# A two-layer FNet/H3 kernel: the work list of the 128-point stage is reordered, its short convolution is spread in even shares, and its constants are loaded one item ahead

## The chip, the cores and the metric

The kernel runs on one core of one Trainium2 chip. The metric is the time of the whole program on the device, in microseconds (us), lower is better. It is given as the median of several runs. One further execution was taken by the profiler, and all durations in this text come from it. The trace names the engines PE (matrix products), PEld (the weight loads beside them), DVE (element-wise work, two inputs), ACT (element-wise work, one input, and copies out of PSUM), POOL (a few very small operations and some DMAs) and SP (most DMAs).

## What is computed

```python
x = A_x                                        # 2048 x 576, f32
x = x + A_ref(layernorm(x), ...)               # y = Re(DFT_seq(DFT_hidden(x)))
x = x + B_ref(layernorm(x), B_k, B_v, ...)     # below
x = x + A_ref(layernorm(x), ...)
x = x + B_ref(layernorm(x), B_k, B_v, ...)

def B_ref(q, k, v, shift_k, ssm_k, ssm_D):
    k_shift = short causal convolution of k over 4 positions, per channel
    kv = k_shift * v
    y = long causal convolution of kv with ssm_k (FFT of 4096 points, per channel)
    return q * (y + kv * ssm_D)
```

The B branch but for its gate `q` doesn't depend on x: `kv` and its long convolution are computed once and used by both layers.

## The kernel before

The program is one unrolled list of instructions per engine. The author writes them in one order; the framework's scheduler may move an instruction within its engine's list, puts in all waits, and after that each engine runs its list strictly in order. An instruction that waits holds everything behind it on that engine; a DMA that waits on SP's list holds the DMAs behind it.

All products are f32 products in three terms: each operand is split into a rounded high part (written by ACT, line 92) and the remainder (a subtraction on DVE, line 93), called hi and lo below.

**Layer 1, A branch** (`layer`, line 296): for each of 4 column blocks and for the cosine and the sine matrix there are 16 steps. A step loads one 128x512 piece of the DFT matrix (`load_c`, line 213), splits it (hi on ACT and lo on DVE, into tiles called `mats`), and issues 14 products of 128x512 into four PSUM banks `s` and one bank `rm`. During the first 16 steps it also needs row block j of the normalised x. Blocks 8 to 15 go through a chain (`sums`, line 612, and `normed_x`, line 638): ACT sums (L615), DVE scales (L616), ACT squares (L617), DVE scales (L618), POOL raises to a power (L619), DVE multiplies (L641), ACT scales (L642), ACT rounds (L195), DVE forms the remainder (L197, L198). After 16 steps the four banks are copied out and split again (tiles `u`).

**The 128-point stage** of the long convolution (`branch`, line 343) is interleaved with these steps by hand: lines 736 to 744 take pieces of it, about two half items per step, until step 42. It works off a list `todo` (lines 394 and 395) of 32 items, (j, 1) for row block j of the kernel `ssm_k` and (j, 0) for row block j of the signal `kv`. For an item

- `f1_loads` (line 398) issues its input from SP (`land`, three tiles) and, if j is new, the constants of j (`fc`, five tiles, 256 KB) from POOL (line 170); it runs two items ahead (line 448);
- `f1_split` (line 415): a signal is first multiplied by v (DVE, line 419); then hi on ACT and lo on DVE (tile `f1r`);
- `f1_products` (line 427): 12 products of 128x288, copied out by ACT (line 436) and stored to DRAM from ACT's list (line 437). From item 8 on the products lag two items behind the split.

The order before is: items (1,1), (0,1), (2,1), (3,1), then signals 0 to 3, then (j,0), (j,1) in turn for j from 4 on.

The signals need the short convolution (`convolve`, line 377), made in pairs of row blocks: a pair is 7 DVE operations on 128x1152 (four products, L386, three additions, L391; a product is cut in two of 128x576 where its rows wrap around). Lines 449 to 456 decide how many of them go out in each half item: what is still owed for the next signal that lacks rows, divided by the halves until then, rounded up.

PSUM has three banks for these products (`bk`). The stage after it (tiles `mid`, from step 45 on) reads back what this stage stored.

Of the kernel before, what the change touches and what calls it, by code (L numbers as in the profile page):

```python
# [12 lines left out]
AF = mybir.ActivationFunctionType  # L13
OP = mybir.AluOpType

P = 128
S = 2048
D = 576
J = S // P
# [8 lines left out]
EARLY = 6  # L28
ROWS = (0, 1, 2, 3, 4, 5, 6, 7, 8, 9)
K_FIRST = 4  # L30
F1_16 = 5
F1_LAG = 8
F1_END = 42
# [32 lines left out]
def fnet_h3_kernel(ctx: ExitStack, tc: tile.TileContext, x, c_mat, w_re, w_im, k_pad, v, shift_k,  # L66
# [101 lines left out]
    def load_fr(dst, src):  # L168
        with tc.issue_after(pows[-1]):
            nc.gpsimd.dma_start(dst, src)  # L170
# [169 lines left out]
    def quads(v):  # L340
        return v.rearrange("p (a q) -> p a q", a=4)

    def branch():
# [33 lines left out]
        def convolve():  # L377
            for i in range(J // 2):
                if not wt:
                    load_w4()  # L380
                load_k(i + KR - 1)
                rp = rows[i] = two(ring["rp"]())
                for t in range(4):
                    out_t = two(tmp) if t else rp
                    for n, k in k_rows(2 * i + t):
                        nc.vector.tensor_tensor(out_t[:, n], k, wt[3 - t][:, n], OP.mult)  # L386
                    yield
                    if t == 1:
                        load_k(i + KR)
                    if t:  # L390
                        nc.vector.tensor_tensor(rp, rp, out_t, OP.add)  # L391
                        yield

        todo = [(1, 1), (0, 1)] + [(j, 1) for j in range(2, K_FIRST)] + [(j, 0) for j in range(K_FIRST)]
        todo += [(j, src) for j in range(K_FIRST, J) for src in range(2)]
        loads = [0]

        def f1_loads(upto):
            while loads[0] < min(upto, len(todo)):
                j, src = todo[loads[0]]  # L400
                loads[0] += 1
                if j not in fcs:
                    fcs[j] = quads(ring["fc"]())
                    if pows:
                        load_fr(fcs[j], f1c[j])
                    else:
                        raw = quads(tmp[:, :4 * P])
                        nc.sync.dma_start(raw, f1c[j])
                        nc.scalar.activation(fcs[j], raw, AF.Copy)
# [27 lines left out]
                nc.scalar.dma_start(t_d[hf][:, j, :, src, :], so)  # L437
                yield

        conv, made_ops, split_up = convolve(), 0, []  # L440
        for n, (j, src) in enumerate(todo):
            f1_loads(n + 1)
            if n < 2:
                yield
            split_up.append((j, src, f1_split(j, src), fcs[j]))
            products = f1_products(*split_up.pop(0)) if len(split_up) > (1 if n < F1_LAG else 2) else iter(())
            if n:
                f1_loads(n + 3)
            later = [m for m in range(n + 1, len(todo)) if todo[m][1] == 0 and 7 * (todo[m][0] // 2 + 1) > made_ops]
            for half in range(2):  # L450
                next(products, 0)
                if later and n > 1:
                    left = 7 * (todo[later[0]][0] // 2 + 1) - made_ops
                    for _ in range(-(-left // (2 * (later[0] - n) - half)) if left > 0 else 0):
                        next(conv)
                        made_ops += 1
                yield
        next(conv, 0)
        for left_over in split_up:
# [646 lines left out]
```

## Time and profile before

| | us |
|---|---|
| runs before: median of 3 (lowest, highest) | 1201.36 (1199.54, 1201.96) |
| the profiled execution, its own time | 1199.98 |
| its span, from first to last instruction | 1198.1 |
| busy PE, DVE, ACT, POOL | 1177.1, 838.9, 633.9, 75.1 |
| the clock that PE was granted | 0.999 |

The profiled execution is 1.4 us faster than the median and inside the range of the runs; 1.9 us of its time lies outside the span. A row of the timeline gives start, duration, engine, line, operation, tiles and the count that was merged, and in brackets the idle time before it and who ended it. PE's products are pipelined, so a row's duration ends after the next one has begun; losses are best read from one start to the next.

### The profile page before, as it was taken

What the parts mean: (1) busy time and instruction counts of PE and PEld (TensorE: products, weight loads), DVE (VectorE), ACT (ScalarE), POOL (GpSimd) and SP (SyncE); (2) the same over time, 40 slices, a digit from 0 to 9 for tenths busy, and PEclk for the clock granted to TensorE, in tenths of its full rate; (3) what the DMA queues carried; (4) which work ended last, traced back from release to release, by engine and by line L of the source; (5) the groups of instructions that cost most, each with busy time, mean ns of one, the idle gap of its engine ahead of it and who ended that gap; (6) DMA issues with size and microseconds to landing.
All of it is one profiled execution on the core that took longest, in us unless ns stands there. A gap on an engine that the chain in (4) does not pass through costs nothing.

```text
span 1198.1 us, 18264 instructions
## 1 busy us (share of the span) xinstructions
PE 1177.1 (98%) x6320; PEld 1026.9 (86%) x6320; DVE 838.9 (70%) x1495; ACT 633.9 (53%) x1266; POOL 75.1 (6%) x116
## 2 busy tenths in 40 slices
PE   7999999999999999999999999999999999999997
PEld 6888888988888888889988898888888888889997
DVE  7889983679877677775447766875676777764764
ACT  7965665467766667665435666544444435440200
POOL 2210000000000000001101121000000000001111
PEclk9999999999999999999999999999999999999999
DMA  9879998546766657658967686872772677794621
GB/s 345 285 241 309 287 288 271 169 128 199 207 191 191 215 164 215 205 141 242 314 203 236 221 258 213 273 259 71 216 272 83 206 277 273 227 353 145 222 88 41
DMA packets 146111, 261.96 MB, mean 219 GB/s; under 512 B 15841, under 2 KB 44769, under 8 KB 146018
## 3 DMA queue, kind: packets, MB, share of 16 engines
q1 hardware_dynamic: 102674, 205.58, 53.9%
q10 hardware_dynamic: 36432, 42.63, 10.2%
q0 software_dynamic: 6912, 12.59, 4.0%
q8 instruction: 50, 0.82, 0.3%
q14 instruction: 43, 0.35, 0.1%
HBM read 194.09 MB, written 66.65 MB: 218 GB/s over the span
## 4 chain that ended last, share of the span: by engine, by line
PE 71%; ACT 3%; DVE 3%; DMA 2%; issue 1%; ACTq 0%; POOLq 0%; DVEq 0%
PE s L75 39%; PE bk L75 28%; PE rm L75 4%; ACT flts L490 2%; ACT mid L490 1%; DMA flts<-in_c_mat 1%; DVE mid L496 1%; DMA flts<-t 1%; DMA flts<-vd 1%; DVE u L93 1%; DMA ph<-in_c_mat 0%; DVE mats L93 0%; ACT mats L92 0%; DVE flts L510 0%; DVE flts L269 0%
## 5 line engine op out<-in xcount | busy, mean ns | idle before, releaser
L75 PE MATMUL s<-mats 128*128 128x512 f32 x2088 | 528.7, 392 | 0.8 <-DVE u L93 0.5
L75 PEld LDWEIGHTS s<-mats 128*128 128x128 f32 x2088 | 380.9, 188 | 70.5 <-DVE u L93 1.3
L92 ACT ACTIVATE mats<-flts 128x512 fp32r<-128x512 f32 x206 | 128.4, 626 | 96.1 <-PE bk L75 32.5
L93 DVE TENSOR_TENSOR mats<-flts,mats 128x512 fp32r<-128x512 f32 x206 | 141.1, 688 | 53.4 <-ACT mats L92 50.8
L490 ACT ACTIVATE flts<-bk 64x288 f32<-64x288 f32 (+1 forms) x288 | 115.9, 406 | 103.1 <-PE bk L75 85.0
L496 DVE TENSOR_TENSOR mid<-flts,mid 128x576 fp32r<-128x576 f32 (+1 forms) x160 | 102.0, 638 | 47.9 <-ACT mid L490 44.0
L75 PE MATMUL bk<-mid 128*128 128x288 f32 x768 | 128.5, 298 | 3.3 <-ACT flts L490 2.2
L75 PEld LDWEIGHTS bk<-mid 128*128 128x128 f32 x768 | 114.8, 188 | 19.6 <-ACT flts L490 8.1
L75 PE MATMUL bk<-w,u 128*128 128x288 f32 x864 | 120.2, 295 | 0.8 <-DVE flts L283 0.7
L75 PEld LDWEIGHTS bk<-w,u 128*128 128x128 f32 x864 | 117.4, 188 | 3.9 <-DVE flts L283 1.5
L490 ACT ACTIVATE mid<-flts 128x576 fp32r<-128x576 f32 (+1 forms) x159 | 87.1, 581 | 14.9 <-DMA flts<-vd 9.6
L75 PE MATMUL rm<-mats 128*128 128x512 f32 x304 | 94.7, 390 | 0.0
L436 ACT ACTIVATE flts<-bk 128x288 f32<-128x288 f32 x128 | 49.0, 410 | 46.5 <-PE bk L75 39.2
L75 PEld LDWEIGHTS bk<-f1r 128*128 128x128 f32 x384 | 59.5, 192 | 14.8 <-ACT f1r L92 6.9
L75 PE MATMUL bk<-f1r 128*128 128x288 f32 x384 | 65.0, 301 | 7.3 <-ACT f1r L92 6.4
L75 PE MATMUL bk<-mats 128*128 128x288 f32 (+1 forms) x376 | 67.8, 317 | 0.0
L75 PEld LDWEIGHTS rm<-mats 128*128 128x128 f32 x304 | 56.9, 188 | 11.8
L283 DVE TENSOR_TENSOR flts<-flts,bk 128x288 f32<-128x288 f32 x48 | 21.8, 453 | 63.8 <-PE bk L75 63.6
L75 PE MATMUL s<-t,mats 128*128 128x512 f32 x264 | 64.9, 389 | 0.0
L184 POOL TENSOR_TENSOR flts<-flts 128x1 f32<-128x1 f32 x35 | 29.6, 845 | 523.8 <-DVE flts L183 523.8
L75 PE MATMUL bk<-mats,t 128*128 128x288 f32 (+1 forms) x368 | 59.3, 303 | 0.0
L75 PEld LDWEIGHTS bk<-mats 128*128 128x128 f32 x376 | 55.6, 188 | 3.4
(148 smaller groups left out, 1429.7 us busy)
## 6 DMA issues: line engine op xcount, KB each, us to landing
flts<-in_c_mat SPq DMA_DIRECT2D x148, 256.0 KB, 3.6
ph<-in_c_mat SPq DMA_DIRECT2D x54, 512.0 KB, 4.2
t<-flts ACTq DMA_DIRECT2D x64, 288.0 KB, 4.4
flts<-t SPq DMA_DIRECT2D x64, 288.0 KB, 3.0
flts<-in_c_mat SPq DMA_DIRECT2D x30, 512.0 KB, 5.1
vd<-flts ACTq DMA_DIRECT2D x64, 144.0 KB, 2.8
flts<-vd SPq DMA_DIRECT2D x32, 288.0 KB, 4.8
mid<-in_i2c POOLq DMA_DIRECT2D x32, 256.0 KB, 4.9
```

What stands on the lines that cost most here:

```text
L75: nc.tensor.matmul(ps, lhsT, rhs, start=first, stop=last, skip_group_check=more)
L92: a = nc.scalar.activation(h, src, AF.Copy).ins
L93: return a, nc.vector.tensor_tensor(l, src, h.bitcast(F32), OP.subtract).ins
L184: pows.append(nc.gpsimd.tensor_tensor(rs, ve, mhalf, OP.pow).ins)
L283: added[:] = [nc.vector.tensor_tensor(r[:, cs], r[:, cs], ps[:, :HD], OP.add).ins]
L436: stored[:] = [nc.scalar.activation(so[:, c, :], ps[:, :HD], AF.Copy).ins]
L490: last_act.append(nc.scalar.activation(*args, **kw).ins)
L496: nc.vector.tensor_tensor(l, src, h.bitcast(F32), OP.subtract)
```

## The change

The list of items, what is loaded when, and the spreading of the convolution are changed. The order of items is now (1,1), (0,1), (2,1), (3,1), (0,0), (1,0), and then for j = 4, 5, ... 15 the kernel item (j,1) followed by the signal item (j-2,0), with signals 14 and 15 at the end. A signal j from 4 on so stands at place 2j+3 of the list, where it stood at 2j; a kernel item j at 2j-2, where it stood at 2j+1. From item 8 on, the constants of the item at hand and of the next one are requested behind the split, and no longer together with the input two items ahead. The convolution gets a running share: the largest debt per half over all coming signals is added at each half, and an operation goes out for each whole unit; a pair may not begin before the signal two pairs back has been used.

```diff
+K_AHEAD = 3
...
-        todo = [(1, 1), (0, 1)] + [(j, 1) for j in range(2, K_FIRST)] + [(j, 0) for j in range(K_FIRST)]
-        todo += [(j, src) for j in range(K_FIRST, J) for src in range(2)]
+        todo = [(1, 1), (0, 1)] + [(j, 1) for j in range(2, K_FIRST)] + [(0, 0), (1, 0)]
+        for j in range(K_FIRST, J):
+            todo += [(j, 1), (j - K_AHEAD + 1, 0)]
+        todo += [(j, 0) for j in range(J - K_AHEAD + 1, J)]
         loads = [0]
+
+        def f1_const(j):
+            if j not in fcs:
+                fcs[j] = quads(ring["fc"]())
+                if pows:
+                    load_fr(fcs[j], f1c[j])
+                else:
+                    raw = quads(tmp[:, :4 * P])
+                    nc.sync.dma_start(raw, f1c[j])
+                    nc.scalar.activation(fcs[j], raw, AF.Copy)
 
         def f1_loads(upto):
             while loads[0] < min(upto, len(todo)):
                 j, src = todo[loads[0]]
                 loads[0] += 1
-                if j not in fcs:
...
+                if j <= K_FIRST:
+                    f1_const(j)
                 landed[j, src] = ring["land"]()
...
-        conv, made_ops, split_up = convolve(), 0, []
+        conv, made_ops, split_up, share = convolve(), 0, [], 0.0
         for n, (j, src) in enumerate(todo):
             f1_loads(n + 1)
             if n < 2:
                 yield
-            split_up.append((j, src, f1_split(j, src), fcs[j]))
+            xf = f1_split(j, src)
+            if n > 7:
+                f1_const(j)
+                if n < len(todo) - 1:
+                    f1_const(todo[n + 1][0])
+            split_up.append((j, src, xf, fcs[j]))
...
                 if later and n > 1:
-                    left = 7 * (todo[later[0]][0] // 2 + 1) - made_ops
-                    for _ in range(-(-left // (2 * (later[0] - n) - half)) if left > 0 else 0):
+                    owed = [(7 * (todo[m][0] // 2 + 1) - made_ops, 2 * (m - n) - half) for m in later]
+                    share += max(left / halves for left, halves in owed)
+                    while share > 0.999 and made_ops < 7 * (J // 2):
+                        pair_at = made_ops // 7
+                        if pair_at > 1 and todo.index((2 * pair_at - 3, 0)) > n:
+                            break
                         next(conv)
                         made_ops += 1
+                        share -= 1
```

The number of instructions stays the same on every engine. What the scheduler makes of it differs from about 30 us of the span on, on PE between its products 112 and 766 of 6320 (up to 161 us); behind that PE's list is the same row by row. Three places follow, as the instructions stand in each engine's list; the new file's lines are one or more higher (L386 is now L387, L391 is L392, L419 is L426, L93 is L94).

First, DVE ahead of the `u` splits of block 0's first half, at 65 to 71 us of the trace. Before:

```order
L198 TENSOR_TENSOR mats<-early,mats 128x512
L93 TENSOR_TENSOR f1r<-f1f,f1r 128x576
L386 TENSOR_TENSOR f1f<-f1f 128x1152
L93 TENSOR_TENSOR mats<-flts,mats 128x512
L391 TENSOR_TENSOR f1f<-f1f 128x1152
L93 TENSOR_TENSOR mats<-flts,mats 128x512 x2
L93 TENSOR_TENSOR u<-s_66,u 128x512
```

and now:

```order
L199 TENSOR_TENSOR mats<-early,mats 128x512
L94 TENSOR_TENSOR f1r<-f1f,f1r 128x576
L94 TENSOR_TENSOR mats<-flts,mats 128x512
L392 TENSOR_TENSOR f1f<-f1f 128x1152
L94 TENSOR_TENSOR mats<-flts,mats 128x512 x2
L94 TENSOR_TENSOR u<-s_66,u 128x512
```

One operation of the convolution has gone from this stretch.

Second, DVE right behind the `u` splits, at 75 to 88 us of the trace. Before:

```order
L419 TENSOR_TENSOR f1f<-f1f,flts 128x576
L386 TENSOR_TENSOR f1f<-f1f 128x1152 x2
L93 TENSOR_TENSOR f1r<-f1f,f1r 128x576
L93 TENSOR_TENSOR mats<-flts,mats 128x512
L391 TENSOR_TENSOR f1f<-f1f 128x1152
L93 TENSOR_TENSOR mats<-flts,mats 128x512
L386 TENSOR_TENSOR f1f<-f1f 128x1152
L419 TENSOR_TENSOR f1f<-f1f,flts 128x576
L391 TENSOR_TENSOR f1f<-f1f 128x1152
L93 TENSOR_TENSOR mats<-flts,mats 128x512
L93 TENSOR_TENSOR f1r<-f1f,f1r 128x576
L386 TENSOR_TENSOR f1f<-f1f 128x576 x2
```

and now:

```order
L94 TENSOR_TENSOR f1r<-flts,f1r 128x576
L387 TENSOR_TENSOR f1f<-f1f 128x1152
L94 TENSOR_TENSOR mats<-flts,mats 128x512
L392 TENSOR_TENSOR f1f<-f1f 128x1152
L94 TENSOR_TENSOR mats<-flts,mats 128x512
L426 TENSOR_TENSOR f1f<-f1f,flts 128x576
L387 TENSOR_TENSOR f1f<-f1f 128x1152 x2
L94 TENSOR_TENSOR f1r<-f1f,f1r 128x576
L94 TENSOR_TENSOR mats<-flts,mats 128x512
L94 TENSOR_TENSOR f1r<-flts,f1r 128x576
L392 TENSOR_TENSOR f1f<-f1f 128x1152
L94 TENSOR_TENSOR mats<-flts,mats 128x512
```

Ahead of the third split of a matrix piece (`mats`) here stood five convolution operations and two products with v; now there are four and one.

Third, DVE in the chain of the normalised row blocks, at 33 to 39 us of the trace (128x1 rows are the chain's scalars, L641 now L658 is the one behind POOL's power). Before:

```order
L618 TENSOR_SCALAR flts<-flts 128x1
L616 TENSOR_SCALAR flts<-flts 128x1
L93 TENSOR_TENSOR f1r<-flts,f1r 128x576
L641 TENSOR_TENSOR flts<-flts 128x1
L391 TENSOR_TENSOR f1f<-f1f 128x1152
L93 TENSOR_TENSOR mats<-flts,mats 128x512
L618 TENSOR_SCALAR flts<-flts 128x1
L386 TENSOR_TENSOR f1f<-f1f 128x1152
L616 TENSOR_SCALAR flts<-flts 128x1
L197 TENSOR_TENSOR mats<-early,mats 128x64
L198 TENSOR_TENSOR mats<-early,mats 128x512
```

and now:

```order
L635 TENSOR_SCALAR flts<-flts 128x1
L392 TENSOR_TENSOR f1f<-f1f 128x1152
L635 TENSOR_SCALAR flts<-flts 128x1
L658 TENSOR_TENSOR flts<-flts 128x1
L633 TENSOR_SCALAR flts<-flts 128x1
L658 TENSOR_TENSOR flts<-flts 128x1
L94 TENSOR_TENSOR mats<-flts,mats 128x512
L635 TENSOR_SCALAR flts<-flts 128x1
L658 TENSOR_TENSOR flts<-flts 128x1
L198 TENSOR_TENSOR mats<-early,mats 128x64
L199 TENSOR_TENSOR mats<-early,mats 128x512
```

Three of the chain's L658 now stand ahead of the row block that these rows end with, where one L641 stood; each waits for POOL.

More of the change, by code (lines that the diff above doesn't have):

```diff
@@ L401, in f1_loads @@
                 loads[0] += 1
-                if j not in fcs:
[L403 to L409, printed above, removed]
+                if j <= K_FIRST:
+                    f1_const(j)
                 landed[j, src] = ring["land"]()
```

## Prediction

> **What bounds the kernel now.** I read the page first (busy time of each engine, then the cost of the products that the change moves), then the stretches by windows, then PE's list of waits, and last PE's timeline, to see what single waits the stage has.
>
> ```profile
> span 1198.1 us, 18264 instructions
> PE 1177.1 (98%) x6320; PEld 1026.9 (86%) x6320; DVE 838.9 (70%) x1495; ACT 633.9 (53%) x1266; POOL 75.1 (6%) x116
> L75 PE MATMUL bk<-f1r 128*128 128x288 f32 x384 | 65.0, 301 | 7.3 <-ACT f1r L92 6.4
> ```
>
> PE is busy for 1177.1 of 1198.1 us, so whatever another engine gains can show only where PE stands still; all its idle time together is 21.0 us. The products of the reordered stage (bk from f1r) have 7.3 us of idle time ahead of them.
>
> ```profile
> PE bk L75 <- ACT f1r L92: 6.4, 2, 5.9
> 32.60:66.20 33.60, 33.60 (x160) 28.24 (x159) 27.34 (x63) 30.34 (x65) 9.61 (x10) 1.00 0.79 254
> 66.20:96.20 30.00, 29.27 (x147) 24.20 (x146) 28.39 (x36) 14.58 (x33) 1.58 (x3) 1.00 0.81 262
> 96.20:126.20 30.00, 30.00 (x165) 26.29 (x164) 29.57 (x33) 18.18 (x42) 1.58 (x3) 1.00 1.01 328
> ```
>
> Of those 7.3 us the first row explains 6.4, and 5.9 of that is one wait: the program's start, before the point from which the lists differ. What is left for this change is small. The windows (their columns are the busy time of PE, PEld, DVE, ACT and POOL, the granted clock, the DMA share and GB/s) cover most of the stretch in which the lists differ: PE counts as idle for only 0.73 us, all of it between 66.2 and 96.2. DVE is what stands behind PE: 28.39 of 30.00 there and 29.57 in the next window. The granted clock is 1.00 throughout, so no term is needed for it.
>
> Idle time as the trace counts it misses what hides in the overlap of pipelined products. So I count from one start to the next.
>
> ```profile
> 67.69 1.22 PE L75 MATMUL bk<-f1r 128*128 128x288 f32 x8
> 68.75 2.00 PE L75 MATMUL s<-mats 128*128 128x512 f32 x8
> 70.59 0.39 PE L75 MATMUL rm<-mats 128*128 128x512 f32 x1
> 71.26 3.01 PE L75 MATMUL s<-mats 128*128 128x512 f32 x12 [0.28 <-DVE u L93]
> ...
> 79.46 1.59 PE L75 MATMUL bk<-f1r 128*128 128x288 f32 x9
> 80.89 2.00 PE L75 MATMUL s<-mats 128*128 128x512 f32 x8
> ...
> 83.18 2.43 PE L75 MATMUL s<-mats 128*128 128x512 f32 x10
> 86.05 0.53 PE L75 MATMUL bk<-f1r 128*128 128x288 f32 x2 [0.44 <-ACT f1r L92]
> 86.42 0.62 PE L75 MATMUL s<-mats 128*128 128x512 f32 x2
> ...
> 94.36 2.38 PE L75 MATMUL bk<-f1r 128*128 128x288 f32 x15
> 96.58 1.08 PE L75 MATMUL s<-mats 128*128 128x512 f32 x4
> ```
>
> The unit of a 128x512 product is (2.43 - 0.39) / 9 = 0.227 us (the row at 83.18: its length less one product's own, over the nine others), and of a 128x288 product (68.75 - 67.69) / 8 = 0.132 us. Against these units the stretch loses in six places that are worth counting: 70.59 to 71.26, 0.67 - 0.227 = **0.44**; inside the row at 71.26, 3.01 - 0.39 - 11 x 0.227 = **0.12**; 79.46 to 80.89, 1.43 - 9 x 0.132 = **0.24**; 83.18 to 86.05, 2.87 - 10 x 0.227 = **0.60**; 86.05 to 86.42, 0.37 - 0.26 = **0.11**; 94.36 to 96.58, 2.22 - 15 x 0.132 = **0.24**. Together **1.8 us**. That is what the change can win directly.
>
> **The change part by part.** No instruction is added or taken away, so the 1177 us of products stay; only places and requests move.
>
> ```profile
> L386 DVE TENSOR_TENSOR f1f<-f1f 128x1152 f32<-128x1152 f32 x5 | 6.7, 1345 | 0.0
> ```
>
> *Even shares of the convolution, and signals later.* This group is of DVE between 66.2 and 96.2 us: one convolution operation takes 1.35 us. Counted in the order of both kernels up to the split that stands at about 96 us in before, DVE has 12 operations' worth of convolution there now and 8 after: 4 x 1.35 = 5.4 us less, in a stretch where DVE's free time is 1.6 us. At the `u` copies (the first place in the section on the change) one operation fewer stands ahead, 1.35 us against a loss of 0.44 + 0.12: both go. What is late next there is ACT's copy of the four banks itself, which ends no later than before.
>
> ```profile
> 69.42 2.07 ACT L92 ACTIVATE u<-s 128x512 fp32r<-128x512 f32 x4 [2.40 <-DVE f1f L391]
> 84.80 0.63 ACT L92 ACTIVATE mats<-flts 128x512 fp32r<-128x512 f32 x1 [2.20 <-DMA flts<-in_c_mat]
> 78.20 0.33 SPq L365 DMA_DIRECT2D f1f<-in_k_pad  x1
> 79.51 2.16 SPq L166 DMA_DIRECT2D flts<-in_c_mat  x2
> ```
>
> The loss at 86.05 (0.60 + 0.11) comes through three queues. PE waits for ACT's f1r; right ahead of that, at 84.80, ACT has a matrix piece for which it stood 2.20 us, since its load hadn't landed; SP could issue that load only at 79.51, because the k_pad load in front of it (78.20) had to wait for a tile that DVE's convolution frees. With DVE 5.4 us lighter the tile is free earlier, and the k_pad load sits further back. I take 0.71 as gone. If that cover fails, it stays, and no more. The two losses on bk's own groups (0.24, 0.24) end on banks that ACT hasn't copied out; ACT is 14.58 of 30.00 busy there and waits for DVE and for loads, so I take them as gone too, though this is the weakest of the terms.
>
> *Order of the items.* A kernel item needs no convolution, so PE has 12 products at hand that depend on SP and ACT and one DVE split alone. Their number to 161 us is the same. Price nothing; hidden under it is the extra lag, which only makes the stored results of signals later by three places. The stage that reads them begins after all of them are issued in both kernels.
>
> *Constants one item ahead.*
>
> ```profile
> 89.40 0.53 POOL L170 DMA_DIRECT2D f1r<-in_f1c  x1 [7.53 <-PE bk L75]
> 99.44 0.53 POOL L170 DMA_DIRECT2D f1r<-in_f1c  x1 [9.51 <-PE bk L75]
> f1r<-in_f1c POOLq DMA_DIRECT2D x15, 256.0 KB, 5.4
> ```
>
> POOL issues a block's constants when PE frees a tile, here 10.0 us apart (89.40 to 99.44), thus 5.0 us per item; they land 5.4 us after the issue. Block j is now requested at item 2j - 3 and first read by the products of item 2j - 2, which lag two items: three items, 15 us, against 5.4. The tile (of five) was last read by signal j - 5, issued five items before that. Nothing waits, price 0. Without this cover one landing of 5.4 us would show at each block; it needs items of under 1.8 us. POOL's only other work in that stretch is the powers below, and the request that moved ahead of three of them costs its 0.53 us in POOL's list, under DVE's work.
>
> *What is put in front of something else.* The third place in the section on the change adds: two more of the chain's waits for POOL stand on DVE ahead of a normalised row block's remainder (L198), and behind it the splits of matrix pieces queue, for which PE waits.
>
> ```profile
> 54.48 0.16 DVE L641 TENSOR_TENSOR flts<-flts 128x1 f32<-128x1 f32 x1 [0.66 <-POOL flts L619]
> 54.69 0.69 DVE L198 TENSOR_TENSOR mats<-early,mats 128x512 fp32r<-128x512 f32 x1
> 56.10 2.45 PE L75 MATMUL s<-mats 128*128 128x512 f32 x10
> 62.23 0.68 DVE L198 TENSOR_TENSOR mats<-early,mats 128x512 fp32r<-128x512 f32 x1
> 64.36 1.75 PE L75 MATMUL s<-mats 128*128 128x512 f32 x7
> ```
>
> A wait for POOL costs DVE 0.66 where nothing stands between; two are 1.32. The block's remainder at 54.69 ends at 55.38 and its first reader is the second product of the row at 56.10, thus at 56.33: a slack of 0.95. At 62.23 it is 64.36 - 62.91 = 1.45. Pushed by 1.32 the first is 1.32 - 0.95 = 0.37 late, the second not. I take **0.4** as added. The ends: 0, since DVE has 33.60 - 27.34 = 6.3 us free in that window and the moved convolution operation (1.35) pays for the push; and 3 x 0.66 = 2.0, if three blocks lose a wait each. I stay near the lower end because its rows are nearest.
>
> **Sum**: -1.8 + 0.4 = -1.4 us. Against the profiled execution's own 1199.98 that is 1198.6. That execution is 1.4 below the median of 1201.36; the same step from the median gives **1199.9**, which I predict.
>
> **The rivals.**
>
> *F, faster.* Two waits behind the stage go as well.
>
> ```profile
> 217.72 0.64 PE L75 MATMUL s<-mats 128*128 128x512 f32 x2
> 218.76 0.92 PE L75 MATMUL bk<-w,u 128*128 128x288 f32 x5 [0.41 <-DVE flts L283]
> PE bk L75 <- DVE flts L283: 0.7, 2, 0.4
> ```
>
> The first, between the two rows, is 1.04 - 2 x 0.227 = 0.59 where the trace counts 0.41 idle; the list of waits has 0.7 for both, so the second (near 224 us) is by the same ratio 0.3 x 0.59 / 0.41 = 0.4, together 1.0. For it: SP's load of the matrix w now stands three places earlier. Against it: every list is the same from 161 us on, and these end on DVE work that follows PE's own pace. With no loss at the row blocks: -1.8 - 1.0 = -2.8, 1198.6.
>
> *N, the change doesn't do what it says.* PE's stalls only change place: the losses on bk's groups and at 86.05 end on loads (2.20 us for in_c_mat) and on banks, and with a DMA share of 1.01 between 96.2 and 126.2 us, the transfers and not DVE may set when those come. Then the 1.8 us appear again as waits for transfers, at 96 to 161 us: 1201.4. Against it: PE counts no idle time in that window.
>
> *S, slower.* The chain of the row blocks becomes what PE waits for, at 33 to 64 us: each of the eight blocks 8 to 15 shows a POOL wait of 0.66 to PE, 8 x 0.66 = 5.3, net -1.8 + 5.3 = +3.5, 1204.9. It decides from the point where the slack of each block is below 0.66. For it: ACT is 30.34 of 33.60 busy in that window, and powers take longer beside DVE:
>
> ```profile
> 36.86 1.59 POOL L619 TENSOR_TENSOR flts<-flts 128x1 f32<-128x1 f32 x1 [2.21 <-DVE flts L618]
> 53.89 0.55 POOL L619 TENSOR_TENSOR flts<-flts 128x1 f32<-128x1 f32 x1 [2.13 <-DVE flts L618]
> 36.70 1.35 DVE L386 TENSOR_TENSOR f1f<-f1f 128x1152 f32<-128x1152 f32 x1
> ```
>
> A power takes 0.55 beside an idle DVE and 1.59 beside a convolution operation. Against it: it then ends at 38.45, 0.40 behind DVE's operation (38.05), so DVE has worked meanwhile and its wait doesn't grow; and the two slacks above are 0.95 and 1.45.
>
> [...]
>
> **How the numbers follow.** Forecast 0.48 (its terms rest on rows of the stretch, but the step is small), F 0.22, N 0.14, S 0.16. About 0.2% of 1201.36, 2.4 us, is what a measurement of this kernel can tell from no change, so faster means below 1198.96 and slower above 1203.76. F lies below; of the forecast, whose runs scatter by half of 1201.96 - 1199.54 = 1.2 us, a quarter (0.12) does too: faster 0.34. S is slower: 0.16. The rest, 0.36 + 0.14, is the same: 0.50. The range takes in F less that scatter, 1198.6 - 1.2 = 1197.4, and, above, the upper end at the row blocks (-1.8 + 2.0, 1201.6) with the same scatter, 1202.8; N lies inside, S is left out with some 0.03 of tails.
>
> **What would show it.** After the change PE's timeline between 66 and 100 us should have no step over 0.1 us above the units; DVE between 75 and 96 us should show convolution operations apart, not two or three together; POOL's waits for PE ahead of its constants should be shorter, and no PE wait should name DMA f1r. The wait for DVE u at 71.26 should be gone. The forecast is wrong if PE shows waits for mats of L198 or L195 (S), if the waits at 218 and 224 us are gone (F), or if new ones stand between 96 and 161 us (N).

## The result and the profile after

| | us |
|---|---|
| before: median of 22 runs (lowest, highest) | 1200.1 (1196.94, 1203.59) |
| changed: median of 22 runs (lowest, highest) | 1196.92 (1194.13, 1201.16) |
| ratio, 95% interval | 0.9976 (0.9969 to 0.9983) |
| changed, the profiled execution: time, span | 1198.31, 1196.5 |

The change makes the kernel faster by 0.24%, 2.9 us (2.0 to 3.7). The prediction was 1.4 us less, 1199.9; the median is 1196.92. The direction was right and the size was not. What failed is the sum: it holds +0.4 at the row blocks that wasn't there, nothing for about 1.1 us outside the reordered stretch, and it starts from a median of three runs (1201.36) that 22 runs put at 1200.1.

The page of the changed kernel, beside that of before, shows the same work and a span that is 1.6 us shorter; the windows, of the same stretches as before, show where PE no longer stands still:

```profile
span 1196.5 us, 18260 instructions
PE 1176.5 (98%) x6320; PEld 1027.8 (86%) x6320; DVE 840.1 (70%) x1495; ACT 636.3 (53%) x1266; POOL 73.0 (6%) x116
```

```profile
32.60:66.20 33.60, 33.60 (x160) 28.25 (x159) 27.85 (x63) 31.34 (x68) 8.42 (x10) 1.00 0.81 260
66.20:96.20 30.00, 30.00 (x156) 25.91 (x155) 28.91 (x36) 17.37 (x38) 1.14 (x3) 1.00 0.92 289
96.20:126.20 30.00, 30.00 (x164) 26.25 (x163) 29.57 (x33) 16.81 (x37) 1.58 (x3) 1.00 0.98 310
```

In the second window PE is busy for all 30.00 us and starts 156 products instead of 147. DVE is as busy as before (28.91 against 28.39, and 29.57 in both kernels in the third). That is the first sign that the forecast's reason, a lighter DVE, is not the whole story.

PE's timeline of the changed kernel, at the places that answer to those shown of before:

```profile
70.16 0.61 PE L76 MATMUL rm<-mats 128*128 128x512 f32 x2
70.61 1.08 PE L76 MATMUL bk<-f1r 128*128 128x288 f32 x7
71.53 2.89 PE L76 MATMUL s<-mats 128*128 128x512 f32 x12
...
83.23 1.52 PE L76 MATMUL s<-mats 128*128 128x512 f32 x6
84.59 0.95 PE L76 MATMUL bk<-f1r 128*128 128x288 f32 x6
85.38 1.53 PE L76 MATMUL s<-mats 128*128 128x512 f32 x6
...
92.02 0.96 PE L76 MATMUL bk<-f1r 128*128 128x288 f32 x6
92.83 1.55 PE L76 MATMUL s<-mats 128*128 128x512 f32 x6
```

Six products of 128x512 in 84.59 - 83.23 = 1.36 are 0.227 each; six of 128x288 in 85.38 - 84.59 = 0.79 are 0.132 each: the units of before. The row at 71.53 follows the seven at 70.61 after 0.92 = 7 x 0.132: the wait for `u` is gone. And the products of this stage stand in groups of three, six and seven, where before had nine and fifteen in a row at these places.

For all kernels below I add up, in such stretches of PE's list, what each start comes later than the unit after the start in front of it ("loss"), by the numbers of the products. Products 111 to 250 run at about 33 to 63 us, 250 to 400 at 63 to 94, 400 to 520 at 94 to 116. Each kernel's own first profile is the first number:

| loss in us, products | 111-250 | 250-400 | 400-520 | 4500-5600 |
|---|---|---|---|---|
| before, four profiles | 0.10, 0.10, 0.63, 0.14 | 1.74, 2.25, 1.49, 0.99 | 0.50, 0.50, 0.50, 0.50 | 1.47, 0.96, 1.33, 1.71 |
| changed, four profiles | 0.07, 0.06, 0.06, 0.06 | 0.20, 0.20, 0.20, 0.21 | 0.31, 0.31, 0.32, 0.31 | 0.70, 0.31, 0.40, -0.11 |

Over products 111 to 520 that is 2.36 in the mean before and 0.58 now: **1.8 us** won where the change acts. Start and stages between scatter by more than that from one execution to the next: the first 111 products lose 3.0 to 5.5 us in these eight profiles, products 1000 to 1200 1.2 to 4.3. The mean span of the four profiles is 1198.0 before and 1195.9 now. A single pair of profiles can't carry a statement about one microsecond of the whole; the stretch can, since it repeats.

### The profile page after: what moved, and what is told of

Same layout as the page of the kernel before. It is cut to its first block, busy times and chain, and to the rows that moved or that the text cites. A ratio compares the mean times of both kernels' runs of the same rounds, so it can differ in the third digit from the quotient of the medians.

```text
span 1196.5 us, 18260 instructions
## 1 busy us (share of the span) xinstructions
PE 1176.5 (98%) x6320; PEld 1027.8 (86%) x6320; DVE 840.1 (70%) x1495; ACT 636.3 (53%) x1266; POOL 73.0 (6%) x116
## 4 chain that ended last, share of the span: by engine, by line
PE 73%; ACT 3%; DVE 3%; DMA 1%; issue 1%; ACTq 0%; POOLq 0%; DVEq 0%
PE s L76 40%; PE bk L76 29%; PE rm L76 4%; ACT flts L507 2%; ACT mid L507 1%; DVE mid L513 1%; DMA flts<-vd 1%; DVE u L94 1%; DMA flts<-in_c_mat 0%; DVE flts L527 0%; DMA flts<-t 0%; DVE flts L270 0%; ACT u L93 0%; ACT mats L93 0%; DVE mats L94 0%
## 5 line engine op out<-in xcount | busy, mean ns | idle before, releaser
L93 ACT ACTIVATE mats<-flts 128x512 fp32r<-128x512 f32 x206 | 128.2, 626 | 97.9 <-PE rm L76 37.0
L94 DVE TENSOR_TENSOR mats<-flts,mats 128x512 fp32r<-128x512 f32 x206 | 141.2, 689 | 53.1 <-ACT mats L93 51.4
```

What stands on the lines that cost most here:

```text
L93: a = nc.scalar.activation(h, src, AF.Copy).ins
L94: return a, nc.vector.tensor_tensor(l, src, h.bitcast(F32), OP.subtract).ins
```

## The experiments

The theory after the result (A): PE's losses at 70 to 95 us end on DVE, which has too much convolution ahead of its splits; the order of the items puts signals off, so that fewer operations stand there. Rivals: the even shares do it (B); the losses come from how PE's own list and the lag are arranged, whatever DVE does (G, H); the rest of the gain lies elsewhere. Times are ratios to the kernel before on the same chip, with the 95% interval.

### The parts alone

**The order alone.** Edit: the convolution's ration and the constants' requests as in before, the list `todo` as in the change. In this kernel and in the one without early constants, block 5's constants are requested into the tile of block 1 before the products of signal 1 are issued, so that signal 1 is multiplied by those of block 5; the amount of work is the same.

```diff
-        todo = [(1, 1), (0, 1)] + [(j, 1) for j in range(2, K_FIRST)] + [(j, 0) for j in range(K_FIRST)]
-        todo += [(j, src) for j in range(K_FIRST, J) for src in range(2)]
+        todo = [(1, 1), (0, 1)] + [(j, 1) for j in range(2, K_FIRST)] + [(0, 0), (1, 0)]
+        for j in range(K_FIRST, J):
+            todo += [(j, 1), (j - K_AHEAD + 1, 0)]
+        todo += [(j, 0) for j in range(J - K_AHEAD + 1, J)]
```

> Only the order of the items is changed; convolution and constants as before. Theory A (the order takes convolution operations from ahead of the splits: DVE's list has 24 of them ahead of the 25th split of a matrix piece, where before has 28 and the whole change has 24): the PE losses of 66 to 100 us go, products 100 to 500 are about 1.7 us shorter than before, and the time is 0.15 to 0.25% below before. Rival B (the even shares carry the gain): within 0.1% of before, losses at 71 and 86 us still there.

Measured: 0.9981 (0.9972 to 0.9991); products 250 to 400 lose 0.47, 400 to 520 0.31. The order alone carries the gain.

**The even shares alone.** Edit, in the kernel before (the piece of the change's diff on the ration):

```diff
-                    left = 7 * (todo[later[0]][0] // 2 + 1) - made_ops
-                    for _ in range(-(-left // (2 * (later[0] - n) - half)) if left > 0 else 0):
+                    owed = [(7 * (todo[m][0] // 2 + 1) - made_ops, 2 * (m - n) - half) for m in later]
+                    share += max(left / halves for left, halves in owed)
+                    while share > 0.999 and made_ops < 7 * (J // 2):
...
```

> Only the even shares of the convolution; order of items and constants as before. Theory A: DVE's list has 14 convolution operations ahead of the u splits and 27 ahead of the 25th split, against 14 and 28 before, so the losses at 71 and 86 us stay: within 0.1% of before. Rival B: 0.15 to 0.25% faster, products 100 to 500 about 1.7 us shorter.

Measured: 0.9996 (0.9987 to 1.0005). Over products 250 to 400 its profile shows 0.79, not the 1.7 that A gave: the wait at 71 us is missing, those at 80, 87 and 95 us are there (0.25, 0.31, 0.24). But PE had lost 2 us more than in the first profile of before by then (first product at 6.72, and 5.85 lost in the first 111 products against 5.91 and 4.84), which DVE could use; a drop of PE's clock is part of it (last section). B is out by the time; that 71 us depends on who is late, PE or DVE, is seen here for the first time.

**Order and constants, without the shares.** Edit: the same piece taken back, in the changed kernel:

```diff
-                    owed = [(7 * (todo[m][0] // 2 + 1) - made_ops, 2 * (m - n) - half) for m in later]
...
+                    left = 7 * (todo[later[0]][0] // 2 + 1) - made_ops
+                    for _ in range(-(-left // (2 * (later[0] - n) - half)) if left > 0 else 0):
```

> The order of the items with the constants one item ahead; the convolution rationed as before. Theory A (the order carries the gain): 12 convolution operations ahead of the u splits as in the whole change (before: 14), the losses of products 250 to 400 fall from 1.7 to 2.2 us to under 0.5, and the time is 0.17 to 0.27% below before. Rival B (the even shares matter beside the order): over 0.1% slower than the whole change.

Measured: 0.9989 (0.9980 to 0.9998), losses 0.14, 0.20 and 0.32 in the three stretches, as in the whole change. The time is 0.11% below before, short of A's 0.17 to 0.27. It is 0.13% above the first timing of the whole change, as B has it, and 0.05% above the second (below), as B has it not, so the time doesn't decide between them. The stretch is the same to 0.1 us: the even shares add nothing there.

**The change without the constants one item ahead.** Edit, in the changed kernel:

```diff
-                if j <= K_FIRST:
-                    f1_const(j)
+                f1_const(j)
...
-            if n > 7:
-                f1_const(j)
-                if n < len(todo) - 1:
-                    f1_const(todo[n + 1][0])
```

> The whole change without the constants one item ahead (requested with the input two items ahead, as before). Every engine's list is then row for row that of the whole change. Theory A: the same time as the whole change (0.24% below before, within 0.1%), and its profile is a second look at the same lists: the 0.6 us by which the whole change's profile starts later, and the 0.6 us more that it waits at 216 to 224 us, are chance of the one execution and differ here. Rival C (the waits at 216 to 224 us are what the change costs): they are about 1.6 us again, against 1.2 before.

Measured: 0.9966 (0.9953 to 0.9979), stretch 0.06, 0.20, 0.32; the waits at 215 to 222 us are 1.2 us, against 1.9 in the first profile of the change and 1.2 in that of before: chance, not a cost (rival C is out). The early requests change no instruction's place in any engine's list, in either order of items; what they change is which products the load of block 5 waits for.

**The whole change and the kernel before again.**

> The whole change once more, timed and profiled. Theory A: products 250 to 400 lose 0.20 us as in the first profile; time 0.15 to 0.3% below before. For the part of the gain that the stretch doesn't explain: if it is systematic, the losses of products 4500 to 5600 (two waits for late loads, at 863 and 1045 us) stay below 1 us and those of the start below 12; if it is chance, they lie among those of the kernels with the old order (0.9 to 2.0 and 10.7 to 12.6).

> The kernel before once more, for a second profile of it and as a measure of scatter. Expected: ratio 1.000 within 0.1%; the six losses between 66 and 100 us (1.75 us in all) are there again within 0.2 us, since they follow from the lists; losses that differ by more than that elsewhere are chance of an execution.

Measured: 0.9984 (0.9975 to 0.9992) for the change, 0.9992 (0.9980 to 1.0003) for before against itself. This second timing of the change is a gain of 1.9 us (1.0 to 3.0), against 2.9 (2.0 to 3.7) in the first. The losses are in the table above. Before's six losses are not as fixed as expected: those at 80 and 95 us come back in all four profiles, the one at 71 us is 0.44, 0.56, 0.75 and 0.38, and the one at 86 us is 0.60, 0.99 and twice nothing (apart from 0.1 behind it in three of them). Two more profiles of each kernel had these expectations:

> A third profile of the kernel before. Theory A: products 250 to 400 lose 1.5 to 2.3 us. If the waits at 863 and 1045 us are systematic they are over 0.9 us together again; if they are chance they may be gone here.

> A third profile of the whole change. Theory A: products 250 to 400 lose 0.2 us. Waits at 863 and 1045 us: under 1 us together if the new kernel systematically has less of them, anything from 0 to 2 if they are chance.

> A fourth profile of the kernel before, for the waits at 863 and 1045 us: 0.6 + 0.7, 0.9 + 0, 0 + 1.3 so far. Over 0.6 in sum if they belong to this kernel, anything from 0 to 2 if they are chance.

> One more profile of the whole change, for the same waits: 0.7 + 0, 0.1 + 0, 0 + 0.3, 0 + 0.8 so far. Under 0.9 in sum if it is systematically better there, anything from 0 to 2 if they are chance.

What the loss at 86 us hangs on can be read by setting the four profiles of before side by side. The first rows are PE's in the second profile, then come ACT's rows ahead of the loss in the second, third and fourth (that of the first, at 84.80, is in the prediction):

```profile
83.46 2.43 PE L76 MATMUL s<-mats 128*128 128x512 f32 x10
86.72 0.53 PE L76 MATMUL bk<-f1r 128*128 128x288 f32 x2 [0.83 <-ACT f1r L93]
```

```profile
85.47 0.63 ACT L93 ACTIVATE mats<-flts 128x512 fp32r<-128x512 f32 x1 [2.59 <-DVE mats L94]
83.85 0.63 ACT L93 ACTIVATE mats<-flts 128x512 fp32r<-128x512 f32 x1 [1.60 <-DMA flts<-in_c_mat]
84.33 0.63 ACT L93 ACTIVATE mats<-flts 128x512 fp32r<-128x512 f32 x1 [0.90 <-DMA flts<-in_c_mat]
```

Three of the four name the load of a matrix piece. The second names a split of DVE, but the four executions run the same lists, and in the first ACT started on this piece at 84.80, while that split still ran, to 84.45 + 0.68 = 85.13:

```profile
78.77 0.68 DVE L93 TENSOR_TENSOR mats<-flts,mats 128x512 fp32r<-128x512 f32 x1
...
84.45 0.68 DVE L93 TENSOR_TENSOR mats<-flts,mats 128x512 fp32r<-128x512 f32 x1
```

So ACT waits for the load each time, and DVE's split only ended by chance at about the same moment. By its semaphore the load is the one that SP issues at 79.51 in the first profile, right behind the end of DVE's split at 78.77 (78.77 + 0.68 = 79.45); the k_pad load, which the prediction named, went out 1.3 us earlier and isn't what holds it. From issue to landing this load took 5.2, 5.6, 4.6 and 3.9 us in the four profiles, and ahead of these products PE lost 0.60, 0.99, 0 and 0. The rows of the second and the fourth:

```profile
flts<-in_c_mat SPq DMA_DIRECT2D x1, 256.0 KB, 5.6
flts<-in_c_mat SPq DMA_DIRECT2D x1, 256.0 KB, 3.9
```

In the changed kernel SP issues the two pieces that answer to those at 79.51 and 81.34 from 76.65 us on:

```profile
76.65 2.20 SPq L167 DMA_DIRECT2D flts<-in_c_mat  x2
```

**The k_pad load later.** Edit, in the kernel before:

```diff
-                    if t == 1:
+                    if t == 3:
                         load_k(i + KR)
```

> The kernel before with one edit: a pair's next k_pad load is issued behind the pair's last addition instead of behind its second, so that SP's list holds the matrix piece's load less long behind it. Theory A: SP's issue of the matrix piece in front of the wait at 86 us comes earlier, ACT's 2.2 us for it shrinks, and PE's loss there (0.6 to 1.1 us in two profiles) falls below 0.2, with the other losses at 71, 80 and 95 us still there: products 250 to 400 lose about 1.0 us instead of 1.7 to 2.2, time 0.05 to 0.1% below before. Rival D (DVE itself is late with that split, and the load's wait hides it): the loss stays at 0.5 or more, ratio 1.000.

Measured: 0.9994 (0.9986 to 1.0003); products 250 to 400 lose 1.73, of it 1.00 at 86 us. The edit moved nothing on SP between 75 and 83 us (k_pad at 77.77, the two matrix pieces at 79.08 and 80.91), so it didn't test what it was made for. The load at 79.08 took 5.6 us to land, and the wait stood. ACT's row ahead of it again names DVE's split, which ended at 84.70, within 0.1 us of the landing. Neither A nor D is decided by it.

### How far ahead, and how much DVE work

**Kernel items two ahead instead of three.** Edit:

```diff
-K_AHEAD = 3
+K_AHEAD = 2
...
-        todo = [(1, 1), (0, 1)] + [(j, 1) for j in range(2, K_FIRST)] + [(0, 0), (1, 0)]
+        todo = [(1, 1), (0, 1)] + [(j, 1) for j in range(2, K_FIRST)] + [(j, 0) for j in range(K_FIRST - K_AHEAD + 1)]
```

> The whole change with kernel items two ahead instead of three (signals 0 to 2 first, then (j,1), (j-1,0)). Theory A (the gain comes from how far the signals are put off): about half of it; products 250 to 400 lose between 0.3 and 1.2 us, time 0.08 to 0.2% below before. Rival E (any alternating order does it): the same as the whole change, 0.24% below before.

Measured: 0.9996 (0.9986 to 1.0007). Products 250 to 400 lose 1.18, and nearly all of it is one wait, for `u`:

```profile
69.56 1.21 PE L76 MATMUL bk<-f1r 128*128 128x288 f32 x8
71.42 2.80 PE L76 MATMUL s<-mats 128*128 128x512 f32 x11 [0.65 <-DVE u L94]
```

1.86 - 8 x 0.132 = 0.80, and 0.11 within the row. DVE's list has 14 operations of the convolution ahead of the `u` splits here, as before; the losses at 80, 86 and 95 us are gone. So the loss at `u` and those behind it have different causes. E is out; the loss is within what A gave, the time, 0.04% below before, is not. (Its profile also holds 1.6 us of a wait at 557 us for a load, see the last experiment.)

**Six products of the convolution doubled**, in the changed kernel.

```diff
-                    for n, k in k_rows(2 * i + t):
+                    for n, k in k_rows(2 * i + t) * (2 if i == 2 or i == 1 and t > 1 else 1):
                         nc.vector.tensor_tensor(out_t[:, n], k, wt[3 - t][:, n], OP.mult)
```

> The whole change with 6 convolution products of pairs 1 and 2 written twice (the same product into the same tile, so the work is DVE's alone: 6 x 1.35 = 8.1 us more). DVE's list then has 13 convolution operations ahead of the u splits (whole change 12, before 14) and 28 ahead of the 25th split of a matrix piece (24, and 28 before); order of items, loads and banks stay. Theory A (what the order buys is DVE's lead): the losses come back, products 250 to 400 lose 0.8 us or more instead of 0.20, and products 400 to 766, where DVE now carries 4 to 6 operations more than before, lose over 1.0 more than the 0.9 of the whole change; time within 0.1% of before or slower. Rival G (the order helps by spreading PE's own groups over banks, whatever DVE does): still 0.15% or more below before.

Measured: 0.9995 (0.9986 to 1.0005), but the losses did not come back: 0.36 in products 250 to 400, 1.10 in 400 to 766 (0.90 in the whole change). PE at `u`:

```profile
70.11 0.39 PE L76 MATMUL rm<-mats 128*128 128x512 f32 x1
70.33 3.03 PE L76 MATMUL s<-mats 128*128 128x512 f32 x12
```

The expectation of A fails in the stretch, and of G in the time. Nothing waits at 80 to 95 us, but the test is weaker there than it looks. The 25th split, ahead of which DVE now has 28 operations as in before, stands only at 101.41 us. Ahead of the three splits that stand at 79, 81 and 84 us in before, DVE's list has 16, 17 and 19 operations of the convolution in before, 13, 14 and 16 in the change, and 14, 15 and 18 here: one or two of three are back. The time is that of before although the stretch isn't. In the one profile, 1.5 us is again one wait at 557 us (products 2600 to 4500 lose 4.55 against 3.0 in the change); whether that wait is what makes the twelve runs longer is not shown.

**Before, with the lag of two items from item 4 on.** PE's list changes widely, DVE's keeps its numbers from the `u` splits on.

```diff
-F1_LAG = 8
+F1_LAG = 4
```

> The kernel before with one number changed: the stage's products lag two items behind the split from item 4 on instead of item 8 on. DVE's list has the same convolution operations ahead of the u splits (14) and of the splits of matrix pieces from the 22nd to the 27th (22, 24, 27, 28, 30, 31). Theory A (DVE's lead): the loss at 86 us stays, products 250 to 400 lose 1.5 to 2.3 us as in the three profiles of before, and the time is that of before. Rival H (before has four signals in a row there, each with its products only one item behind its split; the new order puts kernel items between them): the losses at 80 to 95 us go, the one at 71 us stays, products 250 to 400 lose 0.5 to 1.0, and the time is about 0.1% below before.

Measured: 1.0008 (0.9998 to 1.0018). The losses at 80 and 86 us are gone, with the groups of nine:

```profile
80.92 0.95 PE L75 MATMUL bk<-f1r 128*128 128x288 f32 x6
81.70 1.54 PE L75 MATMUL s<-mats 128*128 128x512 f32 x6
...
84.33 1.55 PE L75 MATMUL s<-mats 128*128 128x512 f32 x6
85.72 0.95 PE L75 MATMUL bk<-f1r 128*128 128x288 f32 x6
```

The loss at 95 us, behind which the list is arranged as before, stays at 0.24. H holds for 80 us, where all four profiles of before lose 0.24. For 86 us this one profile can't tell, since two of the four of before lose next to nothing there either; and the loss at 71 us, which H kept, is missing. No time is won: PE has fewer products of this stage at hand early on and waits for ACT at 54 us (1.10) and for DVE at 66:

```profile
65.67 0.61 PE L75 MATMUL s<-mats 128*128 128x512 f32 x2
67.05 2.60 PE L75 MATMUL s<-mats 128*128 128x512 f32 x10 [0.76 <-DVE mats L198]
```

1.38 - 2 x 0.227 = 0.93 is lost there, at a row block. Products 111 to 520 lose 3.4 together, against 2.36 in the mean of before.

**Sixteen products doubled**, in the changed kernel (pairs 1 to 4).

> The whole change with the convolution's 16 products of pairs 1 to 4 written twice, 16 x 1.35 = 21.6 us more for DVE alone; DVE's list has 15 convolution operations ahead of the u splits and 33 ahead of the 25th split (before: 14 and 28). Theory A: now DVE's lead must be gone, products 250 to 520 lose over 3 us against 0.5 of the whole change. Rival H, in which DVE's lead decides only at the u copies: a loss of about 0.5 at 71 us, and elsewhere losses only once DVE's free time of the stretch (11 us of 128) is used up, from about 100 us on.

Measured: 1.0083 (1.0067 to 1.0099), 10 us slower. PE loses 0.94 at `u` (15 operations ahead), then nothing over 0.3 us until 122 us, and then this:

```profile
122.53 0.40 PE L76 MATMUL rm<-mats 128*128 128x512 f32 x1
124.15 1.66 PE L76 MATMUL s<-mats 128*128 128x512 f32 x6 [1.22 <-DVE mats L94]
...
146.65 2.23 PE L76 MATMUL bk<-f1r 128*128 128x288 f32 x13
155.30 3.78 PE L76 MATMUL s<-mats 128*128 128x512 f32 x8 [6.42 <-DVE u L94]
```

Products 250 to 520 lose 1.75, not over 3. Ahead of the three splits at 79, 81 and 84 us of before, DVE's list now has 16, 17 and 20 operations, as many as before had, and no start between 72 and 107 us comes over 0.1 us late:

```profile
82.82 1.52 PE L76 MATMUL s<-mats 128*128 128x512 f32 x6
84.18 0.42 PE L76 MATMUL bk<-f1r 128*128 128x288 f32 x2
```

One thing isn't put back even here: SP issues the two matrix pieces from 77.42 us on, 2.1 us earlier than in before. As H said, DVE's lead shows at `u` and, apart from that, only when its free time is used up: the second `u` splits come 6.42 us late. 21.6 us more work on DVE cost 10 us; 8.1 us more cost 0.4 in the stretch (0.95 over products 111 to 520, against 0.58), and more than that in time.

**Lag two from item 2 on**, in the changed kernel, aimed at a wait at 28 us.

```diff
-F1_LAG = 8
+F1_LAG = 2
```

> The whole change, with the stage's products lagging two items behind the split from item 2 on instead of item 8 on. It is aimed at the wait near 28 us, which lies ahead of all that the change moves (0.6 to 1.3 us in five of six profiles): there PE has 12 products of this stage in a row and waits for banks that ACT hasn't copied out; now they stand in groups of 5, 3 and 6. If that wait is what scatters and costs: 0.05 to 0.1% faster than the whole change, 0.3% below before. Rival: the wait is the landing of the matrix piece, which the next product then shows: the same as the whole change.

Measured: 0.9993 (0.9983 to 1.0004). The wait at 28 us is still there, 1.26 us by starts against 1.13 in the first profile of the change, now at a smaller group; the rival holds. It is no gain over the change. No kernel of this study is faster than the change by more than the intervals.

**The waits at 863 and 1045 us.** What remains is 4500 to 5600, where all lists are the same. The first rows are of before, the second of the fourth profile of the change, PE at the same products:

```profile
1045.41 0.39 PE L75 MATMUL s<-mats,t 128*128 128x512 f32 x1
1046.35 3.01 PE L75 MATMUL s<-mats,t 128*128 128x512 f32 x12 [0.55 <-DVE mats L93]
```

```profile
1042.28 2.88 PE L76 MATMUL s<-t 128*128 128x512 f32 x12
1045.00 4.24 PE L76 MATMUL s<-mats,t 128*128 128x512 f32 x18
```

The 0.71 us in the first pair is a DVE addition that waits for a load of a matrix piece. The eight profiles with the old order or two ahead lose 0.96 to 2.03 over these products, mean 1.6; the ten with kernel items three ahead -0.11 to 1.44, mean 0.4. That is about 1.1 us, and with the 1.8 of the stretch it is the size of the first timing, 2.9; the second, 1.9, leaves no need for it. The grouping was made after the numbers were seen, and single kernels cross it (1.44 with lag two from item 2 on). It is not explained: at 863 us SP issues the loads at the same distance from the product in all of them (10.8, 9.3, 7.2 and 6.0 us ahead, within 0.4). The waits of 1.5 us at 557 us, for the constants of the later stage, came in 3 of 18 profiles, two of them of kernels whose time equals that of before.

## Why the prediction was right or wrong

- **PE bounds, only its standing counts, the stretch can give 1.8 us**: right. Products 111 to 520 lose 2.36 before and 0.58 after, 1.8 us. The rest beyond that, about 1.1 us of the first timing, the prediction had nowhere. The runs hint at the waits at 863 and 1045 us, and its cause stays open; so does whether it is there at all, since the second timing of the change (1.0 to 3.0) holds 1.8 alone.
- **The base**: 1199.9 was counted from 1201.36, the median of three runs of before. 22 runs give 1200.1, so 1.3 of the 3.0 us between the forecast and the measured 1196.92 is no matter of the change.
- **+0.4 at the row blocks**: wrong, it cost nothing. This is the first mis-sized term: products 111 to 250 lose 0.06 to 0.07, not more than before. The pushed wait and its row block, and the products that read it, in the changed kernel:

```profile
40.66 0.16 DVE L658 TENSOR_TENSOR flts<-flts 128x1 f32<-128x1 f32 x1 [0.66 <-POOL flts L636]
...
40.87 0.69 DVE L199 TENSOR_TENSOR mats<-early,mats 128x512 fp32r<-128x512 f32 x1
```

```profile
41.80 2.43 PE L76 MATMUL s<-mats 128*128 128x512 f32 x10
```

  The wait is there and lasts the 0.66 that the prediction gave it. The block ends at 41.56. The first product of that row for which PE waits for DVE is the third, at 41.80 + 2 x 0.227 = 42.25, and its weights are loaded from 42.03 on (PEld): 42.03 - 41.56 = 0.47, about half a microsecond to spare. The split of a matrix piece behind the block ends at 42.39, only 0.09 ahead of the fourth product, so the push came near to costing something. I had set the whole push against the thinnest slack of before, as if the block and its readers kept their old distance in the new lists.
- **`u` at 71 us: one operation fewer ahead of it**: right in kind; counted from the start of the list it is two fewer, 12 against 14. 14 operations ahead lose 0.5 to 0.9 (before, two ahead), 15 lose 0.94, 12 and 13 lose 0 to 0.26. It is a race with PE: in the shares alone and with the lag from item 4, PE had lost 1 to 2 us before it got there, and 14 lost nothing. With the k_pad load later 14 lost nothing either, and there I don't know why. The row behind this, of DVE in the changed kernel, shows that it now waits for ACT, as the prediction said would be late next:

```profile
69.63 2.48 DVE L94 TENSOR_TENSOR u<-s,u 128x512 fp32r<-128x512 f32 x4 [0.39 <-ACT u L93]
```

- **The two losses of 0.24, at 80 and 95 us, end on banks that ACT hasn't copied, as ACT waits for DVE and for loads**: they went, and they do end on banks: they are 0.24 in all four profiles of before, and the trace names ACT's copy each time. Why ACT is late is wrong: it waits for PE. An item's twelve products fill four banks, and there are three. PE puts one product into each of three banks early, at 77.46 and 78.42, and completes these banks only with the first six of the nine products at 79.46. ACT stands 2.72 us for PE and can start on the first of the three copies only at 79.92; it ends at 80.34, and the seventh of the nine needs that bank. The fifteen at 94.36 do the same. Nine in a row as such don't wait: the nine at 145.84, which are three whole banks, take 1.20 = 9 x 0.133.

```profile
77.46 0.42 PE L75 MATMUL bk<-f1r 128*128 128x288 f32 x2
78.42 0.29 PE L75 MATMUL bk<-f1r 128*128 128x288 f32 x1
...
145.84 1.36 PE L75 MATMUL bk<-f1r 128*128 128x288 f32 x9
147.04 2.91 PE L75 MATMUL s<-mats 128*128 128x512 f32 x12
```

```profile
79.92 1.02 ACT L436 ACTIVATE flts<-bk 128x288 f32<-128x288 f32 x3 [2.72 <-PE bk L75]
```

  So it is how the list opens and closes the banks. With the lag alone changed the one at 80 us went though DVE's list kept its numbers (lag from item 4), and with DVE's operations put back to the numbers of before both stayed away (sixteen doubled).
- **The loss at 86 us (0.71) goes because DVE has 5.4 us less**: it went in every profile with the new order, and the reason is open. The chain that the prediction read, from PE by ACT to a late load, is right; the k_pad load in it is wrong. The load waits for DVE's split and takes 3.9 to 5.6 us to land. In the new order two things change at once: the load goes out earlier (76.65 against 79.51 us), and ACT's list has the split that PE needs next ahead of the awaited piece (at 80.15, for products that start at 84.59), where it stood right behind that piece (at 85.33, for products at 86.05). The lag from item 4 brings only the second (ACT's split at 82.76, products at 85.72) and lost nothing; but that is one profile, and before itself lost 0.1 or less in two of four.
- **Even shares and early constants**: the shares bring nothing that a run shows. The constants bring no time either, price 0 was right, but the new order needs them: without them signal 1 meets the constants of block 5. That POOL's waits for PE would be shorter was wrong, they are 11.31 and 9.11 us at two requests of the changed kernel, and nobody waits for what lands:

```profile
88.47 0.53 POOL L171 DMA_DIRECT2D f1r<-in_f1c  x1 [11.31 <-PE bk L76]
98.11 0.53 POOL L171 DMA_DIRECT2D f1r<-in_f1c  x1 [9.11 <-PE bk L76]
```

- **Rivals**: S (the chain at the row blocks) did not come; N did not, there are no new waits between 96 and 161 us; F's own term (the waits at 218 and 224 us go) did not, they scatter from 1.2 to 4.3 us over products 1000 to 1200 in both kernels. The difference, 2.9 us, came out at F's 2.8, but that is luck: F's zero at the row blocks held, its 1.0 did not, and the time itself lies below F's 1198.6.

## What to carry to other kernels

When an engine fills few output banks, look at which of its products completes a bank, and not at how many stand in a row: three banks opened early and closed late made the fourth wait for a copy (0.24 us), while nine products that close their banks one by one lost nothing (1.20 us for the nine). Before a wait is put down to a busy engine, put the work back (write an idempotent operation twice), and count it at the place of the wait: here the count was taken at a split some 20 us behind it. And when a trace names the engine that ended a wait, look at the same wait in a second execution of the same lists: what had not yet ended there is not the cause. A change of 0.2% needs the same stretch from several profiles; a wait that is 0.6 in one profile was 0.99 in the next and 0 in two others.

## What the hardware showed that I had not expected

One PE wait of 1.16 us was followed by a loss larger than itself, 1.6 us. In the profile of the shares alone PE stood for these 1.16 us near 29 us, and about 2 us later the granted clock fell to half (0.50, the first of the last three numbers of a row):

```profile
29.74 0.67 PE L76 MATMUL bk<-f1r 128*128 128x288 f32 x3 [1.16 <-ACT flts L440]
```

```profile
32.00:35.30 3.30, 3.30 (x10) 2.63 (x10) 3.30 (x5) 2.99 (x8) 0.00 (x0) 0.50 1.04 391
217.70:221.00 3.30, 3.30 (x14) 3.30 (x15) 1.64 (x3) 1.21 (x3) 0.00 (x0) 0.50 0.85 250
```

Products of 128x512 start 0.43 us apart there instead of 0.227, and 1.6 us are lost. Waits of 1.09 and 0.97 us at the same place, in two other profiles, had no such effect. The second row is the fourth profile of the changed kernel, whose longest wait just ahead was 0.71 us; half a clock for 3.3 us is about 1.7 of the 4.3 us that products 1000 to 1200 lost there, so the same kernel may meet the drop or not. In the kernel with sixteen products doubled, the clock fell at 153.0 us, during the wait of 6.42 us: it is 0.90 in the mean over 126 to 161 us. What sets the drops off is not shown: the longest waits just ahead of the first two are 1.16 and 0.71 us, the third came within one of 6.42.
